# A short row block moved to the front of the second MLP, and the planner's keys laid out anew

## The chip, the cores and the metric

The kernel runs on one core of a Trainium2 chip. The metric is device time in microseconds (us) of one execution, the median of several. The engines are named as in the profile: PE is TensorE, which multiplies (PEld is its loading of weights), DVE is VectorE, ACT is ScalarE, POOL is GpSimd and SP is SyncE, whose queue issues nearly all DMAs.

## What is computed

Attention with rotary positions over 4 batches, 8 heads, 576 positions and a head size of 64, then two MLPs over its 2304 rows of 512 values. The change concerns the second MLP.

```python
x = _moe_ref(x, w_in, w_out)                       # first MLP
h = x @ w_in                                       # second MLP: (2304, 512) @ (512, 2048)
g = np.where(h > 0.0, h, np.exp(np.minimum(h, 0.0)) - 1.0)
return g @ w_out                                   # (2304, 2048) @ (2048, 512)
```

## The kernel before, in words

**Numbers in two halves.** Products of float32 matrices are made from float16 halves: each operand is split into a high half (made by ACT) and a low half (made by DVE), and three of the four products of halves are added up in PSUM.

**A planner writes the order.** The code does not issue instructions itself. It records operations with an engine, an estimated cost, the operations they wait for, the buffers they need, and a key. `Plan.run` plays these operations through once, with its own estimates of durations, and on each engine issues next the ready operation with the smallest key. What it writes is fixed: on the chip each engine works through its list in that order, whatever the real durations are. `TUNE` holds the numbers from which the keys are made (`prep`, `va`, `s`, `av`, `w1i` and so on, for parts of the attention and the conversion of weights) and three offsets (`f_dve`, `f_act`, `f_pool`) that decide which engine takes an operation that either could do. Keys of the second MLP are not in `TUNE`, but for `w2i2` and `w2o2`, which set how early the split of its two weight matrices is wanted.

**The second MLP.** Its 2304 rows are done in five row blocks (`NB2 = 5`), of 512 rows but one of 256, in the order that the list `rows` gives. For a block, `block(kb, prev_out)` does this:
- It loads the block's `y` (output of the first MLP) from DRAM, takes its maximum (L1055 on DVE, then L361 and L368 on PE across partitions) and splits it into `yhl` (L1082 on ACT, L1087 on DVE, four of each). There is one `yhl` buffer.
- First product, L1131 on PE: 16 column tiles `u`, each of 12 multiplications as wide as the block. The result of each `u` lies in one of three PSUM buffers `m`. ACT takes the exponential (L1134), DVE does L1138 and L1142, the last of which frees `m`.
- The block with `kb == 0` is done plainly: ACT and DVE split each `u` (L1145, L1149), and the second product is L1258 on PE.
- The other blocks (`fast = kb > 0`) use a scheme with seven products of half size in place of eight (L1207 on PE). It needs sums of the activations (L1114 on DVE, four for each pair of `u`), more splits (L1106 on ACT, L1109 on DVE, three for each pair), and additions behind the products (L1227 on DVE).

**Work that only the fast blocks need.** Seven of the products multiply by sums of the weights. `weight_sums(f)`, recorded right behind block 0 for f = 0 to 7, makes them on DVE (L1005, nine instructions for each f: two 512 wide, six 256 wide, one 1024 wide) with one split on ACT (L1022). They can start when the split of the second weight matrix is done: L514 on ACT and L520 on DVE, 16 of each, in a chain in which each waits for the other. A key of K2+250+f gives the weight sums precedence over the `yhl` of block 1 (key K2+400), and both stand behind the elements of block 0 (keys below zero) wherever those are ready in time.

**What sets the start of a block.** All matmuls of a block stand behind those of the block before it (`prev_out`), but the planner may put L1207 of a block between L1131 of the same block. The first multiplication of a block needs its `yhl`.

Of the kernel before, what the change touches and what calls it, by code (L numbers as in the profile page):

```python
# [20 lines left out]
    s=2, av=1, m=3, E=3, Ehl=3, et=2, qkT=4, R=2, V=1, T=1, v16=4, x=10, t=3, y=1, R2=3, yhl=1, o=3,  # L21
)
TUNE = dict(
    tab=29.669055687884857, f_dve=4735.99490362732, f_act=324.203486712257, f_pool=2991.120911549942, w1i2=87.40583026420265,
    w1o2=-84.0807171361962, dlat=823.3988909607715, kt=434.1730438572996, slack=1000000000.0, w1i=-641.8905164885398,
    w1i_s=35.2508622696485, w1o=-246.81674455296675, w1o_s=7.1899499061784695, prep0_s=62.959721309637985, prep0=574.4583012182783,
    prep=-220.89260578674165, va0=449.5098804882598, va=-814.3532604437504, vs=-249.1490854804778, tiny=688.9344832658534,
    av=505.2864272462129, ex=-841.786808518003, mx=2.580493215482753, s=334.76728659580453, tr=1002.6372188507788, w2i2=-170.54943633953243,
    w2o2=-1595.7316624510645, pt=748.6446072069625, pv=498.37407629952327,
)  # L30
LAT = {"pe": 230.0, "act": 170.0, "dve": 145.0, "pool": 200.0, "dma": 0.0, "none": 0.0}
ORDER = ("pe", "act", "dve", "pool", "dma", "none")
# [187 lines left out]
def kernel(  # L220
# [14 lines left out]
    NT, DM = out.shape  # L235
# [312 lines left out]
    tab = w2i_flat[:, 3 * QW:3 * QW + 27 * HALF]  # L548
# [407 lines left out]
    NB2 = (NT + 511) // 512  # L956
# [10 lines left out]
    def second_mlp(opened, after1, dead, scored):  # L967
# [309 lines left out]
            return prev_out  # L1277

        rows = [512] * (NB2 - 1)
        rows.insert(3, NT - 512 * (NB2 - 1))  # L1280
        done = [after1]
        for kb in range(NB2):
            done = block(kb, done)
# [28 lines left out]
    opened = op({"none": 0}, open2, list(x_ready.values()) + [o for o in W1i.ready + W1o.ready], 0)  # L1312
    dead = [o for hp in range(NP) for o in qk_ready[B - 1, hp] + [v_ready[B - 1, hp]]]
    second_mlp(opened, prev, dead, scored)

    with tc.manual_schedule():
# [55 lines left out]
```

## Time and profile before

| what | value |
|---|---|
| median of 3 runs | 1026.08 us (1023.97 to 1027.85) |
| the profiled execution, time | 1024.77 us |
| its span, first to last instruction | 1023.0 us |
| PE busy | 973.3 us |
| DVE busy | 852.3 us |
| ACT busy | 611.1 us |
| start of the first multiplication of block 0 of the second MLP | 654.70 us |

The profiled execution's own time lies 1.31 us below the median, and 1.8 us above its span. A share of busy time is a mean over stages: the second MLP takes the last third of the span, and within it each block has its own limit. So the views below are by stretch and in order of time.

### The profile page before, as it was taken

The page shows a single profiled execution, that of the slowest core. Times are in us where ns is not written, and L with a number is a line of the kernel's source. Part 1 is how long each engine was busy: PE and PEld are TensorE (multiplying, and loading weights), DVE is VectorE, ACT ScalarE, POOL GpSimd, SP SyncE. Part 2 cuts the span into 40 slices and gives each one's busy share as a digit, 9 for nine tenths or more (in the row PEclk, how much of TensorE's full clock was granted, in tenths as well). Part 3 has the DMA queues.
Part 4 walks back from the last instruction along what each step waited for, and adds up shares of the span by engine and source line. Part 5 has one row for each costly group of instructions (what it writes and reads, how often), then busy time and mean ns, then how long its engine had stood idle before and what let it go on. Part 6 is the DMA issues. An engine that isn't in the chain of part 4 may idle for free. (4 is left out here: it accounts for less than half of the span.)

```text
span 1023.0 us, 19959 instructions
## 1 busy us (share of the span) xinstructions
PE 973.3 (95%) x7818; PEld 691.4 (68%) x7818; DVE 852.3 (83%) x1686; ACT 611.1 (60%) x1184; POOL 0.4 (0%) x6
## 2 busy tenths in 40 slices
PE   3578999999999999999999999999999999998998
PEld 2455787877766678766688778644446846886477
DVE  7999998887997689999885988699698489386982
ACT  4998996565786566786563777474264155062640
POOL 0000000000000000000000000000000000000000
PEclk8579999999999999999999999999999999999999
DMA  8961548887767956778684174000100200102001
GB/s 281 314 211 43 126 70 154 164 144 110 139 114 135 176 92 119 137 159 174 139 161 139 42 214 157 27 1 0 42 1 27 57 1 12 47 7 63 1 11 33
DMA packets 200254, 103.39 MB, mean 101 GB/s; under 512 B 164064, under 2 KB 189280, under 8 KB 200160
## 3 DMA queue, kind: packets, MB, share of 16 engines
q1 hardware_dynamic: 199872, 101.62, 44.5%
q8 instruction: 61, 1.00, 0.4%
q10 hardware_dynamic: 288, 0.51, 0.2%
q14 instruction: 33, 0.27, 0.1%
HBM read 53.46 MB, written 9.44 MB: 61 GB/s over the span
## 5 line engine op out<-in xcount | busy, mean ns | idle before, releaser
L938 PE MATMUL m<-ghl,wo 128*128 128x256 f16 (+3 forms) x1728 | 199.9, 274 | 0.2 <-DVE wo L520 0.2
L1131 PE MATMUL m<-yhl,w2i 128*128 128x512 f16 (+1 forms) x960 | 188.2, 358 | 0.2
L901 PE MATMUL m<-x,wi 128*128 128x256 f16 (+3 forms) x1584 | 187.2, 271 | 1.0 <-DVE t L907 0.9
L938 PEld LDWEIGHTS <-wo 128*128 128x128 f16 x1728 | 157.0, 98 | 41.7 <-issue 11.9
L901 PEld LDWEIGHTS <-wi 128*128 128x128 f16 x1728 | 155.7, 98 | 43.5 <-issue 14.5
L1131 PEld LDWEIGHTS <-w2i 128*128 128x128 f16 x960 | 93.9, 98 | 92.9 <-issue 0.7
L720 ACT ACTIVATE E<-s,st 128x576 f32<-128x576 f32 x144 | 106.6, 741 | 52.5 <-DVE st L716 49.8
L716 DVE TENSOR_REDUCE st<-s 128x1 f32<-128x576 f32 x144 | 106.7, 748 | 4.2 <-PE s L711 4.1
L742 DVE SCALAR_TENSOR_TENSOR Ehl<-E,st,Ehl 128x576 f16<-128x576 f32 x124 | 99.5, 810 | 11.0 <-ACT Ehl L736 10.3
L736 ACT ACTIVATE Ehl<-E,st 128x576 f16<-128x576 f32 x90 | 68.3, 773 | 44.2 <-DMA et<-Ehl 15.2
L1134 ACT ACTIVATE e<-m,y_c 128x512 f32<-128x512 f32 (+1 forms) x80 | 50.9, 639 | 65.0 <-issue 35.6
L711 PE MATMUL s<-qkT 64*128 64x288 f32 (+1 forms) x480 | 81.1, 449 | 1.5 <-ACT E L720 1.4
L1207 PEld LDWEIGHTS <-g 128*128 128x128 f16 x714 | 70.3, 99 | 9.4 <-issue 0.7
L1227 DVE SCALAR_TENSOR_TENSOR x<-z,eo,x 128x256 f32<-128x256 f32 x46 | 22.0, 482 | 51.8 <-PE z L1207 51.6
L916 ACT ACTIVATE ghl<-t 128x320 f16<-128x320 f32 (+3 forms) x96 | 49.8, 524 | 21.1 <-DVE t L907 20.6
L904 ACT ACTIVATE t<-m,hsc 128x320 f32<-128x320 f32 (+3 forms) x96 | 55.5, 578 | 9.0 <-PE m L901 8.1
L711 PEld LDWEIGHTS s<-qkT 64*128 64x128 f32 (+1 forms) x480 | 42.3, 184 | 23.7 <-issue 8.3
L1207 PE MATMUL z<-wo,g 128*128 128x256 f16 x504 | 58.0, 277 | 0.0
L907 DVE SCALAR_TENSOR_TENSOR t<-t,m 128x320 f32<-128x320 f32 (+3 forms) x96 | 52.3, 547 | 5.4 <-ACT t L904 5.2
L1142 DVE SCALAR_TENSOR_TENSOR e<-m,y_c,e 128x512 f32<-128x512 f32 (+1 forms) x80 | 55.1, 690 | 0.4
L919 DVE SCALAR_TENSOR_TENSOR ghl<-t,ghl 128x320 f16<-128x320 f32 (+3 forms) x96 | 52.2, 550 | 2.2 <-ACT ghl L916 2.0
L1106 ACT ACTIVATE g<-R,y_c 128x1024 f16<-128x1024 f32 (+1 forms) x32 | 33.3, 1041 | 24.0 <-DVE R L1114 24.0
(190 smaller groups left out, 1375.8 us busy)
## 6 DMA issues: line engine op xcount, KB each, us to landing
ghl<-in_moe_w_in_dram SPq DMA_DIRECT2D x16, 512.0 KB, 6.2
R<-in_moe_w_out_dram SPq DMA_DIRECT2D x16, 512.0 KB, 4.2
wo<-in_moe_w_out_dram SPq DMA_DIRECT2D x14, 512.0 KB, 4.8
w2i<-in_moe_w_in_dram SPq DMA_DIRECT2D x14, 512.0 KB, 4.2
w2i<-in_k_dram SPq DMA_DIRECT2D x16, 256.0 KB, 3.0
w2i<-in_q_dram SPq DMA_DIRECT2D x16, 256.0 KB, 3.8
w2i<-in_v_dram SPq DMA_DIRECT2D x4, 1024.0 KB, 7.2
R<-y_d SPq DMA_DIRECT2D x8, 512.0 KB, 3.8
```

The costliest lines, as they stand in the source:

```text
L711: nc.tensor.matmul(o, X[r, t:t + (TAIL if h is None else P)], X[r, NS * w:NS * w + NS], start=True, stop=True)
L716: nc.vector.tensor_reduce(out=st["t"][:, a:a + 1], in_=take(hS[a])[:, :, 0:NS], axis=AX.XY, op=ALU.max, negate=True)
L720: nc.scalar.activation(out=take(hE[a]).rearrange("p (c f) -> p c f", c=2), in_=take(hS[a])[:, :, 0:NS], func=AF.Exp, bias=t[:, a:a + 1], s ...
L736: nc.scalar.activation(out=X16[:, 0:S], in_=take(hE[a]), func=AF.Copy, scale=r)
L742: nc.vector.scalar_tensor_tensor(out=X16[:, S:2 * S], in0=E, scalar=r, in1=X16[:, 0:S], op0=ALU.mult, op1=ALU.subtract)
L901: nc.tensor.matmul(ps, W1i.lhs(kk, u, wl), x[:, xl, 0:N], start=kk == 0 and i == 0, stop=kk == KD - 1 and i == 2)
L904: nc.scalar.activation(out=flat(ht), in_=flat(hM), func=AF.Tanh, scale=hsc[b][:, 1:2])
L907: nc.vector.scalar_tensor_tensor(out=flat(ht), in0=flat(ht), scalar=1.0, in1=flat(hM), op0=ALU.add, op1=ALU.mult)
L938: nc.tensor.matmul(ps[:, 0:N], W1o.lhs(f, d, wl), (gh, gl)[xl][:, f, g0:g0 + N], start=f == 0 and i == 0, stop=f == KF - 1 and i == 2)
L1131: nc.tensor.matmul(ps[:, 0:n], W2i.lhs(kk, u, wl), Y[:, xl, kk, 0:n], start=kk == 0 and i == 0, stop=kk == KD - 1 and i == 2)
L1142: nc.vector.scalar_tensor_tensor(out=t[:, 0:n], in0=take(hM)[:, 0:n], scalar=st["c"][:, 0:1], in1=t[:, 0:n], op0=ALU.mult, op1=ALU.max)
L1207: nc.tensor.matmul(ps, AT[A](p, gi, P * tt), BT[B](p, wl), start=p == 0 and i == 0, stop=p == 7 and i == 2)
```

## The change

The list `rows` was 512, 512, 512, 256, 512 and becomes 256, 512, 512, 512, 512. So the short block is now the plain one, and four blocks of 512 rows go through the fast scheme in place of three of 512 and one of 256. Nothing else of the code differs but 27 of the 29 numbers in `TUNE`, of which the diff here shows the first two lines.

```diff
 TUNE = dict(
-    tab=29.669055687884857, f_dve=4735.99490362732, f_act=324.203486712257, f_pool=2991.120911549942, w1i2=87.40583026420265,
-    w1o2=-84.0807171361962, dlat=823.3988909607715, kt=434.1730438572996, slack=1000000000.0, w1i=-641.8905164885398,
+    tab=-225.85054553600983, f_dve=10711.990370883193, f_act=461.965463073505, f_pool=1613.197066616173, w1i2=141.63957986767508,
+    w1o2=-371.9002375178363, dlat=823.3988909607715, kt=223.51619677805178, slack=1000000000.0, w1i=-701.3096471146007,
...
@@ -1277,7 +1277,7 @@
         rows = [512] * (NB2 - 1)
-        rows.insert(3, NT - 512 * (NB2 - 1))
+        rows.insert(0, NT - 512 * (NB2 - 1))
         done = [after1]
         for kb in range(NB2):
             done = block(kb, done)
```

On DVE, in the first product of block 0, the order was this (names are tiles; the number behind a name tells its generation, `m` is PSUM, `e` an activation, `g` its split):

```order
L1138 TENSOR_SCALAR e_8409<-e_8409 128x512
L1149 SCALAR_TENSOR_TENSOR g_8394<-e_8387,y_c,g_8394 128x512
L1142 SCALAR_TENSOR_TENSOR e_8409<-m_8374,y_c,e_8409 128x512
L1138 TENSOR_SCALAR e_8433<-e_8433 128x512
L520 SCALAR_TENSOR_TENSOR w2o<-w2o,w2o_s 128x512
L1142 SCALAR_TENSOR_TENSOR e_8433<-m_8396,y_c,e_8433 128x512
```

In the same place it is now this:

```order
L1138 TENSOR_SCALAR e_8459<-e_8459 128x256
L1149 SCALAR_TENSOR_TENSOR g_8424<-e_8416,y_c,g_8424 128x256
L1142 SCALAR_TENSOR_TENSOR e_8459<-m_8426,y_c,e_8459 128x256
L1149 SCALAR_TENSOR_TENSOR g_8424<-e_8439,y_c,g_8424 128x256
L1138 TENSOR_SCALAR e_8482<-e_8482 128x256
L520 SCALAR_TENSOR_TENSOR w2o<-w2o,w2o_s 128x512
L1142 SCALAR_TENSOR_TENSOR e_8482<-m_8446,y_c,e_8482 128x256
```

The element work of block 0 has half its width, and the work on weights (L520 here) stands between it as before, at its old width.

On DVE around the last of the four L1087, which completes the `yhl` of block 1, the order was this:

```order
L1005 TENSOR_TENSOR wo<-R_8840,wo 128x1024
L1087 SCALAR_TENSOR_TENSOR yhl_8721<-R_8151,ys_s,yhl_8721 128x512
L1005 TENSOR_TENSOR wo<-R_8858,wo 128x1024
L1005 TENSOR_TENSOR e_8912<-w2o 128x512
L1005 TENSOR_TENSOR R_8913<-e_8912 128x256
```

and it is now this:

```order
L1005 TENSOR_TENSOR wo<-R_8826,wo 128x1024
L1087 SCALAR_TENSOR_TENSOR yhl_8701<-R_8046,ys_s,yhl_8701 128x512
L1005 TENSOR_TENSOR wo<-R_8847,wo 128x1024
L1005 TENSOR_TENSOR e_8881<-w2o 128x512
L1005 TENSOR_TENSOR R_8882<-e_8881 128x256
```

The last L1087 stood behind six complete weight sums and all but the last step of a seventh; behind it one more was to be started. It stands now behind five and all but the last step of a sixth, and two are to be started behind it.

On DVE at the first elements of block 1 the order was this, with the last instruction of the weight sums ahead of the first element:

```order
L1005 TENSOR_TENSOR R_8913<-R_8913,w2o 128x256
L1005 TENSOR_TENSOR wo<-R_8913,wo 128x1024
L1138 TENSOR_SCALAR e_9024<-e_9024 128x512
L1142 SCALAR_TENSOR_TENSOR e_9024<-m_8994,y_c,e_9024 128x512
L1109 SCALAR_TENSOR_TENSOR ghl<-e_9024,y_c,ghl 128x256
```

and it is now this:

```order
L1005 TENSOR_TENSOR R_8882<-R_8882,w2o 128x256
L1142 SCALAR_TENSOR_TENSOR e_8900<-m_8868,y_c,e_8900 128x512
L1138 TENSOR_SCALAR e_8926<-e_8926 128x512
L1005 TENSOR_TENSOR R_8903<-w2o,R_8903 128x256
L1005 TENSOR_TENSOR R_8903<-R_8903,w2o 128x256
```

The last two weight sums have moved into the element work of block 1.

## Rows read from the trace of the kernel before

**Rows 1.** The page's head: span, then busy time of each engine.
```profile
span 1023.0 us, 19959 instructions
PE 973.3 (95%) x7818; PEld 691.4 (68%) x7818; DVE 852.3 (83%) x1686; ACT 611.1 (60%) x1184; POOL 0.4 (0%) x6
```

**Rows 2.** Busy time by stretch: length, each engine's us (instructions), PE clock, DMA share, GB/s.
```profile
0.00:100.00 100.00, 64.19 (x496) 43.80 (x497) 89.28 (x171) 78.99 (x158) 0.44 (x6) 0.78 0.67 217
100.00:654.70 554.70, 547.54 (x4987) 418.61 (x4984) 481.57 (x930) 377.35 (x789) 0.00 (x0) 1.00 0.66 133
654.70:696.10 41.40, 41.40 (x193) 18.78 (x192) 39.02 (x70) 28.09 (x42) 0.00 (x0) 1.00 0.01 4
895.50:925.40 29.90, 26.61 (x238) 22.98 (x236) 27.61 (x89) 18.39 (x41) 0.00 (x0) 1.00 0.08 23
925.00:930.00 5.00, 4.56 (x27) 3.46 (x28) 1.44 (x3) 0.45 (x2) 0.00 (x0) 0.66 0.30 65
```

**Rows 3.** The chain that ended last, in order: start, us, engine and line.
```profile
654.70 41.44 PE m L1131 x192
696.13 41.44 PE z L1258 x192
737.58 41.44 PE m L1131 x192
...
816.52 41.44 PE m L1131 x192
...
895.47 2.63 PE m L1131 x24
...
941.43 41.44 PE m L1131 x192
982.87 36.70 PE z L1207 x336
```

**Rows 4.** Timeline of DVE: start, us, instruction, idle before it and what ended it.
```profile
646.06 0.75 DVE L520 SCALAR_TENSOR_TENSOR w2o<-w2o,w2o_s 128x512 f16<-128x512 f32 x1 [0.48 <-ACT w2o L514]
...
657.39 0.75 DVE L520 SCALAR_TENSOR_TENSOR w2o<-w2o,w2o_s 128x512 f16<-128x512 f32 x1 [0.79 <-ACT w2o L514]
658.06 0.42 DVE L1138 TENSOR_SCALAR e<-e 128x512 f32<-128x512 f32 x1
...
726.52 0.75 DVE L1087 SCALAR_TENSOR_TENSOR yhl<-R,ys_s,yhl 128x512 f16<-128x512 f32 x1
...
740.97 0.43 DVE L1138 TENSOR_SCALAR e<-e 128x512 f32<-128x512 f32 x1 [6.26 <-ACT e L1134]
...
788.56 1.28 DVE L1109 SCALAR_TENSOR_TENSOR g<-R,y_c,g 128x1024 f16<-128x1024 f32 x1 [1.22 <-ACT g L1106]
...
897.38 0.29 DVE L1138 TENSOR_SCALAR e<-e 128x256 f32<-128x256 f32 x1 [1.38 <-ACT e L1134]
```

**Rows 5.** DVE groups by shape, whole span: count, busy us, mean ns, idle before.
```profile
L1142 DVE SCALAR_TENSOR_TENSOR e<-m,y_c,e 128x512 f32<-128x512 f32 x64 | 47.6, 744 | 0.4
L1138 DVE TENSOR_SCALAR e<-e 128x512 f32<-128x512 f32 x64 | 26.8, 418 | 11.7 <-ACT e L1134 11.7
L738 DVE TENSOR_SCALAR Ehl<-E,st 128x576 f16<-128x576 f32 x34 | 17.5, 517 | 5.0 <-DMA et<-Ehl 4.4
L1149 DVE SCALAR_TENSOR_TENSOR g<-e,y_c,g 128x512 f16<-128x512 f32 x16 | 11.9, 742 | 0.0
L1005 DVE TENSOR_TENSOR e<-w2o 128x512 f32<-128x512 f16 x16 | 11.0, 687 | 0.3
L1005 DVE TENSOR_TENSOR wo<-R,wo 128x1024 f16<-128x1024 f32 x8 | 9.7, 1217 | 1.1 <-ACT wo L1022 1.1
L1142 DVE SCALAR_TENSOR_TENSOR e<-m,y_c,e 128x256 f32<-128x256 f32 x16 | 7.4, 476 | 0.0
L1138 DVE TENSOR_SCALAR e<-e 128x256 f32<-128x256 f32 x16 | 4.4, 284 | 1.9 <-ACT e L1134 1.9
L1109 DVE SCALAR_TENSOR_TENSOR g<-e,y_c,g 128x256 f16<-128x256 f32 x6 | 2.9, 476 | 0.0
```

More of the change, by code (lines that the diff above doesn't have):

```diff
@@ L23 @@
 TUNE = dict(
-    tab=29.669055687884857, f_dve=4735.99490362732, f_act=324.203486712257, f_pool=2991.120911549942, w1i2=87.40583026420265,
-    w1o2=-84.0807171361962, dlat=823.3988909607715, kt=434.1730438572996, slack=1000000000.0, w1i=-641.8905164885398,
[L26 to L29, printed above, removed]
+    tab=-225.85054553600983, f_dve=10711.990370883193, f_act=461.965463073505, f_pool=1613.197066616173, w1i2=141.63957986767508,
+    w1o2=-371.9002375178363, dlat=823.3988909607715, kt=223.51619677805178, slack=1000000000.0, w1i=-701.3096471146007,
+    w1i_s=35.295006560150384, w1o=-288.970382295607, w1o_s=7.0294735729774125, prep0_s=80.73354021978547, prep0=711.5060984569377,
+    prep=-518.3682961524775, va0=564.1241425353367, va=-514.3532604437504, vs=-194.15244992060525, tiny=667.6726656029264,
+    av=375.7219813841871, ex=-948.7649659643791, mx=2.67698772504311, s=338.5026763982299, tr=970.8000049482956, w2i2=-219.0150182370548,
+    w2o2=-1719.6996793582275, pt=688.6530860848909, pv=337.7031782414163,
 )
```

## The prediction

> **What bounds the kernel now.** I read the page's head first: PE is busy for 95% of the span, DVE for 83% [rows 1]. Then the busy time by stretch. In the first 100 us PE is busy for 64.2 us and DVE for 89.3, so work that feeds PE sets the pace there. From 100 us to 654.7, where the second MLP begins, PE is idle for 7.2 us of 554.7 [rows 2]. Then the chain that ended last: from 654.70 it is PE almost without a break, with one exception [rows 3]. Block 0 takes 82.88 us (654.70 to 737.58), block 1 takes 78.94 (to 816.52), block 2 takes 78.95, the short block 3 takes 45.96 (895.47 to 941.43), and block 4's multiplications end 78.14 us after it begins, at 1019.57 [rows 3]. Half of a block of 512 would be 39.5, so the short block lost some 6 us. The stretch shows how: from 895.5 to 925.4 DVE is busy for 27.6 of 29.9 us and PE for 26.6 [rows 2]. In that block DVE was the limit.
>
> DVE is close to being the limit elsewhere too. In the first product of block 0 it is busy for 39.0 of 41.4 us while PE never waits [rows 2]. It does the elements of block 0 from 658.06 and between them the split and the sums of the second weight matrix. The last L1087, on which block 1 waits, starts at 726.52, some 10 us before PE comes for it at 737.58 [rows 3, 4]. The reader is to see that this margin exists only because PE takes 82.88 us over block 0.
>
> **The change part by part.** All times of the second MLP count from T, the first multiplication of block 0 (654.70 before), and the sum is made against the profiled execution's 1024.77 us.
>
> *PE's own work.* The plain block of 256 rows needs 192 multiplications of 256 columns (24 of them took 2.63 us, so 21.0) and 96 of 512 columns (192 took 41.44, so 20.7) [rows 3]: 41.8 us in place of 82.88. The fourth fast block of 512 rows takes 78.94 in place of 45.96. Together 120.7 in place of 128.8: a gain of 8.1 us, if nothing waits.
>
> *DVE's work in block 0.* At half width L1138 goes from 418 to 284 ns and L1142 from 744 to 476. L1149 at 256 columns does not occur; the same operation of L1109 at that width takes 476 against its 742 [rows 5]. That saves 0.67 us for each of 16 column tiles, 10.7 us of durations. The work on weights does not shrink: the eight sums cost the same whatever the block's width. So DVE's load falls by far less than PE's 41 us.
>
> *When is the `yhl` of block 1 done?* DVE's list is fixed, and the first element of block 0 needs PE's first result. In the short block of before, that L1138 started 1.9 us after the first multiplication (897.38 against 895.47) [rows 3, 4]. Ten of the L520 stand ahead of it. Before, the chain of L520 and L514 advanced by one in (657.39 - 646.06)/7 = 1.6 us [rows 4], so ten need 16 us. Their scale is wanted by PE after 24 of the 192 L938 of the last block of the first MLP, some 18 us before T, so this just fits and I charge nothing; if it doesn't, the start slips by a microsecond or two. From the first L1138 to the last L1087 the new list has 107 instructions: 48 for the elements of block 0, 6 L520, 4 L1087, 49 of the weight sums. Their durations, each by its group of the view by shape, sum to 54.6 us. DVE's instructions overlap a little at their ends, and some wait for ACT. Before, from the first L1138 to the last L1087, the same kind of list summed to 74.1 us and took 69.2 (658.06 to 727.27) [rows 4], a ratio of 0.934. So the last L1087 ends at T + 1.9 + 51.0 = T + 52.9. PE has finished block 0 at T + 41.8 and waits **11.1 us**, where it had 10 us in hand.
>
> *Inside block 1.* The list goes on with what is left of the weight sums (11.5 us of durations) and the fast elements of block 1 (52.0 us), 63.5 in all. Before, these 52.0 took 48.9 us (740.97 to 789.84) [rows 4], 0.94 with their waits, so DVE now needs 59.7 and is done at T + 112.6. PE cannot run ahead: three buffers `m` are freed only by L1142. After DVE's last split, PE still has 222 of the 336 L1207 (0.109 us each by 36.70/336 [rows 3]) and one exchange across partitions, 0.8 us more (78.94 - 41.44 - 36.70): 25.0 us. Block 1 ends at T + 137.6, which is 84.7 after its start in place of 78.94: **5.8 us** more.
>
> *After that* three fast blocks follow as before, 78.95, 78.95 and 78.14. The multiplications end at T + 373.7; before it was T + 364.87. In sum -8.1 + 11.1 + 5.8 = **+8.8 us**. For bounds I take the ratio of elapsed time to durations from 0.91 (hardly a wait) to 0.97 (most instructions depend on the one ahead): +5.6 to +12.6.
>
> *The first part*, with its keys laid out anew. The number of multiplications on PE is the same. DVE gets rid of 4.5 us of durations in all (five L738 of 517 ns [rows 5] among them), which ACT takes over. Summed in the same way, DVE's list up to the 16th maximum of scores is 3.9 us shorter, but up to the last split of the first weight matrix 5.9 longer. So T moves by between -4 and +6. PE's idle 7.2 us after the first 100 us leave little to gain there [rows 2]. I take -1.
>
> *DMAs.* Two more stores of the output are issued, because the blocks meet the batches at other rows; like the others they lie beside PE. The loads of `y` for block 1 are wanted before T either way. I charge nothing; a late load would delay L1055 and add to the wait above.
>
> *PE's clock.* When PE resumed after the waits of the short block (3.3 us together), the clock was 0.66 of full speed from 925 to 930 us, where the two levels are 1.2 and 2.4 GHz; the price was 0.34 of 4.56 us, 1.5 us [rows 2]. After a wait of 11 us the same must be expected. But block 1's first column tile at half speed takes 5.2 us, and DVE still has the end of one weight sum and the beginnings of two to do (5.7 us of durations, 5.3 elapsed) before it looks at that tile, so I charge nothing. The Trainium skill (TensorE: Matmul & The Clock Gate, Part 1) says that the array's clock falls to the lower level when the engine idles and comes back as it works. The trace agrees with its 0.66; by the page the change adds one more such stretch.
>
> So 1024.77 + 8.8 - 1 = 1032.6 for an execution like the profiled one. The median of the runs shown is 1.3 above it, which gives 1034.
>
> **The rivals.** *PE is the bound and DVE keeps up (faster).* Then only the 8.1 us count, and the time is 1024.77 - 8.1 - 1 + 1.3 = 1017. For it speaks PE's 95% [rows 1]. It decides itself at the last L1087: if its end comes before T + 41.8, the gain is whole. That needs 11 of DVE's 51 us to vanish; nothing in the list before it is optional, and the first element can't start before T. Chance 6%. The Trainium skill (Perfetto Trace Analysis, Identifying the Most-Contended Engine) takes the engine with the highest occupancy as the one to optimize; by that rule this rival would be the forecast. The stretch 895.5 to 925.4, with DVE at 92% and PE waiting, speaks against reading it over the whole span.
>
> *The new keys give back what the blocks lose (no change).* If the first 100 us, where PE idles for 35.8 [rows 2], shrink by 5 us or more, or DVE's ratio is at its low end and T at -4, the time is 1022 to 1031, say 1028. For it: the shorter list up to the 16th maximum. Against it: the longer one to the last split. Chance 23%.
>
> *The waits feed each other (slower still).* If PE stays at the lower clock in block 1, its first product takes up to 82.9 us in place of 41.44 and becomes the limit again; a third of it at that level adds 14, of which the 5.8 us of waiting are cover. That gives 1042. Against it: from 895.5 to 925.4 PE waited a little again and again, and its clock was 1.00 [rows 2]. Chance 13%. My forecast has 58%.
>
> **How the numbers follow.** The likeliest case gives 1034. The range goes down to 1025, which takes in most of the second rival, and up to 1042, which holds the upper bounds of DVE's ratio and of T (+12.6 and +4). A measurement can tell about 0.5% from no change, 5 us: faster below 1021, slower above 1031. Faster has the first rival and a little of the second, 0.08. The forecast lies for its larger part above 1031, and with the third rival slower has 0.67. No measurable change has 0.25.
>
> **What would show it.** Right: PE idle for about 11 us ahead of the first L1131 of block 1, ended by DVE L1087; block 1 some 85 us long with DVE busy for nearly all of its first 60; no wait in the four fast blocks' rows of L1207 after that; T within 4 us of 654.7; a clock below 1.00 where PE resumes. Wrong: the last L1087 of block 1 before the last L1258, or a T that has moved by more than the blocks have. In the first case the sum of DVE's list is wrong, in the second the keys of the attention decide the sign.

## The result, and the profile after

| | before | after |
|---|---|---|
| median | 1026.96 us (1023.97 to 1027.95, 4 runs) | 1032.99 us (1031.84 to 1033.85, 4 runs) |
| profiled execution: time, span | 1024.77, 1023.0 us | 1033.85, 1032.1 us |
| T, first multiplication of block 0 of the second MLP | 654.70 | 658.25 |
| last multiplication ends | T + 364.87 | T + 370.39 |

The ratio is 1.0075, with a 95% interval of 1.0055 to 1.0095: the changed kernel is slower, by about 6 us of the medians. The forecast was 1034. In the profiled executions the second MLP has grown by 5.5 us and the part ahead of it by 3.55. These 9.1 us are more than the 6.0 between the medians: the profiled execution after is the slowest of its four, the one before lies 2.2 us below its median.

The page's head shows nearly nothing, in the form of [rows 1]: PE is still busy for 95% of the span and DVE for 83%.

```profile
span 1032.1 us, 20140 instructions
PE 975.7 (95%) x7890; PEld 701.0 (68%) x7890; DVE 858.7 (83%) x1687; ACT 616.1 (60%) x1191; POOL 0.4 (0%) x6
```

The chain that ended last, as in [rows 3], gives the blocks: T, then the starts of blocks 2, 3 and 4 and the end.

```profile
658.25 1.32 PE m L1131 x12
...
792.61 41.44 PE m L1131 x192
...
871.56 41.44 PE m L1131 x192
...
950.51 41.44 PE m L1131 x192
991.95 36.69 PE z L1207 x336
```

From block 2 on every block takes 78.95 us and the end comes 236.03 us after 792.61, as PE's own work asks. So all that the second MLP loses lies ahead of T + 134.36. PE's timeline shows where (start, us, instruction, count, idle before it and what ended it):

```profile
700.61 2.32 PE L1131 MATMUL m<-yhl,w2i 128*128 128x512 f16 x10
...
710.05 19.08 PE L1131 MATMUL m<-yhl,w2i 128*128 128x512 f16 x74 [7.12 <-DVE yhl L1087]
...
747.71 7.93 PE L1131 MATMUL m<-yhl,w2i 128*128 128x512 f16 x36 [1.24 <-DVE e L1142]
...
767.81 5.63 PE L1207 MATMUL z<-wo,g 128*128 128x256 f16 x50 [0.60 <-DVE g L1109]
```

Block 0 is done at 700.61 = T + 42.4. PE runs ten multiplications of block 1 with the quarters of `yhl` that are there, then stands for 7.12 us until the last L1087. DVE's timeline has the other side:

```profile
660.10 0.29 DVE L1138 TENSOR_SCALAR e<-e 128x256 f32<-128x256 f32 x1 [0.47 <-ACT e L1134]
...
709.26 0.74 DVE L1087 SCALAR_TENSOR_TENSOR yhl<-R,ys_s,yhl 128x512 f16<-128x512 f32 x1
...
766.48 1.27 DVE L1109 SCALAR_TENSOR_TENSOR g<-R,y_c,g 128x1024 f16<-128x1024 f32 x1
```

The busy time by stretch (columns as in [rows 2]) closes it: from its first L1138 to the last L1087, and from there to the last split of block 1, DVE is busy for 48.69 of 49.90 and 57.06 of 57.75 us. It waits for nobody; PE waits for it.

```profile
0.00:100.00 100.00, 65.86 (x490) 45.69 (x492) 85.87 (x166) 79.05 (x157) 0.44 (x6) 0.81 0.68 217
100.00:658.25 558.25, 549.17 (x4992) 419.56 (x4989) 482.08 (x935) 383.74 (x803) 0.00 (x0) 1.00 0.65 131
660.10:710.00 49.90, 42.31 (x282) 27.32 (x280) 48.69 (x108) 26.43 (x48) 0.00 (x0) 0.96 0.03 11
710.00:767.75 57.75, 55.73 (x300) 29.92 (x299) 57.06 (x110) 30.63 (x44) 0.00 (x0) 0.95 0.01 3
700.00:725.00 25.00, 17.88 (x70) 7.39 (x69) 24.14 (x49) 9.33 (x13) 0.00 (x0) 0.80 0.05 20
```

### The profile page after: what moved, and what is told of

Its sections match the earlier page's. It is cut to its first block, busy times and chain, and to the rows that moved or that the text cites. A ratio compares the mean times of both kernels' runs of the same rounds, so it can differ in the third digit from the quotient of the medians.

```text
span 1032.1 us, 20140 instructions
## 1 busy us (share of the span) xinstructions
PE 975.7 (95%) x7890; PEld 701.0 (68%) x7890; DVE 858.7 (83%) x1687; ACT 616.1 (60%) x1191; POOL 0.4 (0%) x6
## 4 chain that ended last, share of the span: by engine, by line
PE 68%; DVE 19%; DMA 7%; ACT 3%; issue 2%; SPq 1%; ACTq 0%; DVEq 0%
PE m L938 15%; PE z L1207 14%; PE m L1131 13%; PE m L901 12%; PE s L711 6%; PE av L833 3%; DMA et<-Ehl 3%; DVE st L716 2%; DMA w2i<-in_v_dram 2%; DVE R L1005 2%; DVE Ehl L742 1%; DVE e L1142 1%; PE m L599 1%; DVE t L907 1%; PE av L843 1%
## 5 line engine op out<-in xcount | busy, mean ns | idle before, releaser
L1131 PE MATMUL m<-yhl,w2i 128*128 128x512 f16 (+1 forms) x960 | 191.4, 361 | 9.1 <-DVE yhl L1087 7.1
L901 PEld LDWEIGHTS <-wi 128*128 128x128 f16 x1728 | 156.0, 98 | 42.7 <-issue 13.6
L1131 PEld LDWEIGHTS <-w2i 128*128 128x128 f16 x960 | 94.6, 99 | 104.0 <-issue 14.2
L736 ACT ACTIVATE Ehl<-E,st 128x576 f16<-128x576 f32 x95 | 72.5, 773 | 31.4 <-DMA et<-Ehl 13.6
L1207 PEld LDWEIGHTS <-g 128*128 128x128 f16 x816 | 79.6, 98 | 10.7 <-DVE g L1109 0.9
L1227 DVE SCALAR_TENSOR_TENSOR x<-z,eo,x 128x256 f32<-128x256 f32 x52 | 24.8, 482 | 54.4 <-PE z L1207 54.3
L1207 PE MATMUL z<-wo,g 128*128 128x256 f16 x576 | 64.4, 273 | 0.6 <-DVE g L1109 0.6
L907 DVE SCALAR_TENSOR_TENSOR t<-t,m 128x320 f32<-128x320 f32 (+3 forms) x96 | 52.2, 546 | 5.8 <-ACT t L904 5.5
L1142 DVE SCALAR_TENSOR_TENSOR e<-m,y_c,e 128x512 f32<-128x512 f32 (+1 forms) x80 | 54.9, 690 | 0.3
L919 DVE SCALAR_TENSOR_TENSOR ghl<-t,ghl 128x320 f16<-128x320 f32 (+3 forms) x96 | 52.2, 549 | 3.3 <-ACT ghl L916 3.1
L1207 PEld LDWEIGHTS <-ghl 128*128 128x128 f16 x480 | 46.6, 98 | 6.7 <-issue 0.2
```

Of the source, the lines that this page charges most:

```text
L736: nc.scalar.activation(out=X16[:, 0:S], in_=take(hE[a]), func=AF.Copy, scale=r)
L901: nc.tensor.matmul(ps, W1i.lhs(kk, u, wl), x[:, xl, 0:N], start=kk == 0 and i == 0, stop=kk == KD - 1 and i == 2)
L907: nc.vector.scalar_tensor_tensor(out=flat(ht), in0=flat(ht), scalar=1.0, in1=flat(hM), op0=ALU.add, op1=ALU.mult)
L1131: nc.tensor.matmul(ps[:, 0:n], W2i.lhs(kk, u, wl), Y[:, xl, kk, 0:n], start=kk == 0 and i == 0, stop=kk == KD - 1 and i == 2)
L1142: nc.vector.scalar_tensor_tensor(out=t[:, 0:n], in0=take(hM)[:, 0:n], scalar=st["c"][:, 0:1], in1=t[:, 0:n], op0=ALU.mult, op1=ALU.max)
L1207: nc.tensor.matmul(ps, AT[A](p, gi, P * tt), BT[B](p, wl), start=p == 0 and i == 0, stop=p == 7 and i == 2)
```

## The experiments

The theory: PE's work beside which DVE splits and sums the second weight matrix has been halved, that work of DVE has not, and PE waits for the difference. The rivals: the new keys, PE's clock, the order in which DVE does its work, the form of the short block.

Read from the profiled execution of each kernel, in us from that kernel's own T. Medians and ratios against the kernel before stand with each experiment; a difference to the changed kernel compares medians of different series of runs, in which the kernel before had medians from 1024.95 to 1026.96 us.

| kernel | T | last `yhl` of block 1 done | last split of block 1 done | block 2 begins | multiplications end |
|---|---|---|---|---|---|
| before | 654.70 | 72.6 | 135.1 | 161.8 | 364.9 |
| after | 658.25 | 51.8 | 109.5 | 134.4 | 370.4 |
| e1, row order alone | 655.70 | 52.2 | 110.0 | 143.3 | 379.3 |
| e3, half of the sums | 660.58 | 38.6 | 94.2 | 120.7 | 356.7 |
| e4, `yhl` first | 660.24 | 31.2 | 102.7 | 136.7 | 372.7 |
| e5, second half on POOL | 657.99 | 35.6 | 99.2 | 137.2 | 373.3 |
| e9, the same, all sums early | 655.79 | 39.2 | 112.4 | 139.8 | 375.8 |
| e10, more on POOL, all early | 657.70 | 42.7 | 116.4 | 141.3 | 377.3 |
| e11, on POOL, last four early | 656.09 | 35.5 | 110.0 | 134.8 | 370.9 |

**The two parts of the change apart.**

```diff
 e1: TUNE as before
-        rows.insert(3, NT - 512 * (NB2 - 1))
+        rows.insert(0, NT - 512 * (NB2 - 1))
 e2: TUNE as after, rows.insert(3, ...) as before
```

> The short block comes first, and all keys of TUNE stay as before. Theory (the row order costs about 5.5 us by DVE's work on weights, the new keys 3.5 us by the attention): the first multiplication of block 0 stays at 654.7 us (within 1), PE waits 7 to 11 us ahead of block 1 for the last L1087, and the time is 1024.8 + 5.5 to 7, that is 1030 to 1032, a ratio of 1.005 to 1.007. DVE's list from its first L1138 to the last L1087 of block 1 sums to 55.4 us of durations here (54.6 in the changed kernel), with 11 of the L520 in it in place of 6. Rival 1 (the whole loss comes from the keys): 1017, as if PE's own work counted alone. Rival 2 (the keys were laid out for this row order and without them it is worse): over 1035, by the five additional L520 in block 0.

> The new keys with the old row order. Theory: the first multiplication of block 0 comes at about 658.3 us as in the changed kernel, the second MLP takes as long as before from there (multiplications end 364.9 us after it), so the time is 1028 to 1029, a ratio of 1.003 to 1.004. DVE's list from its first L1138 to the last L1087 of block 1 sums to 72.4 us (74.1 before), so PE does not wait for it. Rival (the 3.5 us belong to the row order, not to the keys): 1025, ratio 1.000.

Measured: e1 1041.03 us against 1026.32, ratio 1.014 (1.0118 to 1.0163); e2 1026.25, ratio 1.0009 (0.9992 to 1.0026). The first theory of the split is wrong in both halves; rival 2 of e1 and the rival of e2 came true. The row order alone costs 14.7 us and not 6, and the keys alone cost nothing that can be measured, so the 3.55 us ahead of T are not theirs as a price. With the short block first the keys win back 8.9 us of the second MLP (379.3 against 370.4 in the table). PE's timeline of e1 has a wait that the changed kernel has not:

```profile
707.98 7.67 PE L1131 MATMUL m<-yhl,w2i 128*128 128x512 f16 x26 [8.45 <-DVE yhl L1087]
...
770.78 0.59 PE L1207 MATMUL z<-wo,g 128*128 128x256 f16 x2 [5.75 <-ACT wo L1022]
...
772.04 5.15 PE L1207 MATMUL z<-wo,g 128*128 128x256 f16 x25 [0.67 <-DVE wo L1005]
```

In e1 five more L520 stand in DVE's list from the first L1138 of block 0 on, and four steps of the first weight sum that the changed kernel has ahead of it. (A weight sum f needs only the slices f and f + 8 of the split, not all 16, so it can start this early.) DVE is at its last split of block 1 as early as in the changed kernel (T + 110.0 and T + 109.5), but nine L1005 of the last sums come behind it, the last ending at T + 116.3, and PE's seven products need them. So the new keys act through what they leave for DVE to do behind T.

**DVE's amount, without its order or PE's work.**

```diff
 e3: each weight sum without T2 and T4
-            o = op({"dve": 4 * c_dve(QD)}, second, [o], k, use=[hs, hd], port=True)
-            o = op({"act": c_act(1024)}, hi, [o], k, use=[hs])
-            t_ops.append(op({"dve": c_dve(1024)}, lo, [o], k, use=[hs], port=True))
+            o = op({"act": c_act(512)}, hi, [o], k, use=[hs, hd])
+            t_ops.append(op({"dve": c_dve(512)}, lo, [o], k, use=[hs], port=True))
```

> The changed kernel with half of DVE's weight sums left out: of each of the eight sums only two of the four parts are made (and split), so T2 and T4 hold old weights and the second MLP's output is wrong where they are used. PE's instructions are the same. DVE loses about 20 us of durations: from its first L1138 to the last L1087 of block 1 its list sums to 41.8 us in place of 54.6, and to the last split of block 1 to 58.5 more in place of 64.4. Theory (DVE's amount of work beside the halved block 0 is what PE waits for): the last L1087 ends at T + 1.9 + 38 = T + 40, PE's wait ahead of block 1 shrinks from 7.1 to at most 1 us, block 1 takes 79 us, and the second MLP is 13 us shorter than in the changed kernel: about 1020, below the kernel before, ratio 0.995. Rival (PE's clock or its own work sets the time of block 1): the time stays within 2 us of the changed kernel, 1031 to 1033.

Measured: 1019.46 us, ratio 0.9928 (0.9904 to 0.9951), 13.5 us below the changed kernel. In the whole second MLP PE waits for nothing (the view of waits has no row), and the chain is PE alone:

```profile
660.58 19.68 PE m L1131 x180
...
702.30 41.44 PE m L1131 x192
...
781.25 41.44 PE m L1131 x192
...
980.58 36.70 PE z L1207 x336
```

The second MLP takes 356.70 us, 8.2 less than before. That is the gain of PE's own work that the change would have brought. Up to the last split of block 1 DVE's list is 18.7 us shorter here (41.8 and 58.5 in place of 54.6 and 64.4); ACT's split of the sums is half as wide too. The rival that PE's own work sets the time of block 1 falls with it: PE has the same multiplications, a few of them in another order. Its clock stays at 1.00 through the second MLP of e3, where PE does not wait, so what a lower clock would cost is not settled here but by DVE's idle time (see the part on the prediction).

**DVE's order, without its amount.**

```diff
 e4:
-            k = K2 + 250 + f
+            k = K2 + 450 + f
```

> The changed kernel with the key of the weight sums raised above that of the yhl of block 1, so that DVE makes the yhl first and the weight sums after it; nothing is left out. From its first L1138 to the last L1087 of block 1 DVE's list now sums to 34.1 us in place of 54.6, and from there to the last split of block 1 to 78.1 in place of 64.4. Theory (the amount of DVE's work counts, not its order): the wait of 7.1 us ahead of block 1 goes, but the last split of block 1 still comes at T + 1.9 + 0.91 x 112 = T + 104 (109.5 in the changed kernel), and two weight sums stand behind it, so PE waits inside block 1 instead and the second MLP gains 0 to 5 us: 1027 to 1033. Rival (the order of the L1087 behind the weight sums is the cause): PE never waits, block 1 takes 79 us, and the time is about 1020.

Measured: 1037.05 us, ratio 1.009 (1.0065 to 1.0114): 4 us above the changed kernel, though the intervals of the two ratios overlap, and its second MLP is 2.3 us longer. That is outside both expectations, if nearer to the theory's. The `yhl` is there 20 us earlier and PE does not wait for it. The view of waits shows what came in its place (us in total, times, longest):

```profile
PE m L1131 <- DVE e L1142: 6.2, 5, 2.3
PE z L1207 <- ACT wo L1022: 4.8, 1, 4.8
PE z L1207 <- DVE wo L1005: 2.0, 2, 1.3
```

Of these 13.0 us 12.4 lie inside block 1, in place of 7.1 ahead of it and 2.0 inside. So the place of the L1087 behind the weight sums is not the cause; what was missed is the same as in e1: ten steps of the last two sums stand behind the last split.

**A part of the sums on POOL.** POOL is idle in the second MLP, and e3 says what 18.7 us less on DVE's list is worth.

```diff
 e5: base after; e5b: the same on base e1
-            o = op({"dve": 4 * c_dve(QD)}, second, [o], k, use=[hs, hd], port=True)
+            o = op({"pool": 4 * c_pool(QD)}, second, [o], k, use=[hs, hd], port=True)
 e9: e5, and
-            k = K2 + 250 + f
+            k = -8.5e4 + f
 e10: e9, and lo (1024 wide) on POOL
 e11: e5, and
-            k = K2 + 250 + f
+            k = K2 + 250 + f if f < 4 else -8.5e4 + f
```

> The changed kernel, complete, with four of the nine instructions of each weight sum (the four 256 wide of its second half) on POOL, which is idle there, in place of DVE. DVE's list from its first L1138 to the last L1087 of block 1 sums to 34.1 us in place of 54.6. Theory (PE waits for the amount of DVE's work): the last L1087 ends by T + 35, ahead of the end of block 0 at T + 42, there is no wait ahead of block 1, and the time is that of the kernel with half of the sums left out, 1019 to 1022, ratio 0.993 to 0.996. No row of the traces so far prices a tensor_tensor on POOL; it fits if the 32 instructions take under about 1.6 us each (51 us). Rival (POOL is slow, or slows DVE while it works): PE waits at the first L1207 that multiplies by the sums, or DVE's rows of 512 and 1024 columns grow above 687 and 1217 ns, and the time is 1030 or more.

> The same move of work to POOL with the short block first and the old keys. With the row order alone the old keys cost 8 us against the new ones. Theory (the keys matter only through what DVE has to do beside block 0 and block 1: five L520 and the last weight sum): with DVE relieved the difference between old and new keys goes, and the time is within 3 us of the variant with the new keys, 1018 to 1023. Rival (the new keys do something for this row order that has nothing to do with DVE's amount): 1027 to 1030.

> The changed kernel with the second half of each weight sum on POOL, as before, and the key of the weight sums lowered to -8.5e4, ahead of the sums of activations (L1114) that took the R2 buffers from the last two of them; no weight sum stands behind block 1's elements now. DVE's list sums to 35.8 + 69.2 us from its first L1138 to the last split of block 1. With the 6.3 us by which its rows grew beside POOL that is 111.3, by 0.91 elapsed 101, so the last split comes at T + 103 and block 1 ends 25 us later at T + 128, against T + 134.4 in the changed kernel. Theory (the last two sums were late because of their place in the list, and the sum of DVE's work then sets the end): 1025 to 1029, no wait for L1022 or L1005 above 1 us. Rival (DVE and POOL disturb each other wherever the sums stand): 1033 or more.

> As the one above, with the last step of each weight sum (1024 wide, 1.22 us on DVE) on POOL too. DVE's list sums to 33.6 + 62.6 = 96.2 us; with 6 to 12 us of growth beside POOL 102 to 108, elapsed 93 to 98, so its last split comes at T + 95 to T + 100, where PE needs it at T + 96. Theory (the amount on DVE): block 1 ends at T + 121 to T + 125, the second MLP takes 357 to 361 us, 1018 to 1023, ratio 0.992 to 0.997. Rival (POOL's wide step holds the R2 buffers longer, and PE waits for the last sums at L1207): 1028 or more. No row prices the 1024-wide step on POOL; by the 0.8 us for 256 columns it would take some 3 us.

> The changed kernel with the second half of each weight sum on POOL, and the early key of -8.5e4 only for the last four sums, so that the split of the second weight matrix (L520) keeps its place ahead of them. DVE's list sums to 34.1 + 70.9 us, with 6.3 of growth beside POOL 111, elapsed 101: its last split comes at T + 103, block 1 ends 25 us later at T + 128, and three blocks of 78.9 to 78.1 follow. Theory (once neither the split nor the sums are late by their place, the amount on DVE alone sets the end): the second MLP takes 364 us, no wait for L520, L1022 or L1005 above 2 us, 1024 to 1029, ratio 0.998 to 1.003. Rival (POOL beside DVE costs more than the rows of before show): 1033 or more.

Measured: e5 1038.98 us, ratio 1.0119 (1.0098 to 1.014); e5b 1046.28, 1.019 (1.0167 to 1.0213); e9 1040.44, 1.014 (1.0118 to 1.0161); e10 1041.2, 1.0143 (1.0121 to 1.0166); e11 1035.83, 1.0108 (1.0091 to 1.0126). All five theories missed: none is faster than the changed kernel, and the difference between old and new keys did not go with the work on POOL (e5b is 7.3 us above e5). The times of the rivals came true in e5, e9, e10 and e11, though e10's not by its mechanism: PE waits there for L1142 and not for the last sums. e5b is above its rival too: sixteen steps of the sums stand behind its last split of block 1, ten in e5, and PE waits 20.0 us for L1022 and L1005.

The table and the waits show two reasons. In e5 the `yhl` is early and there is no wait ahead of block 1, but the last two sums stand behind block 1's own sums (L1114), which have the smaller key and use the same buffers, and PE waits for them at L1207 (7.13 us for the L1022 of one, 4 more behind it). In e9 nothing is late in block 1, which takes 78.95 us, but the early sums stand ahead of the split L520, and block 0 waits, for 12.7 us in all:

```profile
700.32 0.59 PE L1258 MATMUL z<-w2o,g 128*128 128x512 f16 x1 [4.83 <-DVE w2o L520]
...
706.07 0.58 PE L1258 MATMUL z<-w2o,g 128*128 128x512 f16 x1 [3.93 <-DVE w2o L520]
...
711.83 4.78 PE L1258 MATMUL z<-w2o,g 128*128 128x512 f16 x13 [3.94 <-DVE w2o L520]
```

e11 has neither fault, and its second MLP is as long as the changed kernel's (370.9 against 370.4). Yet DVE's last split comes at T + 110.0, as in the changed kernel, with 13.6 us of work (32 x 0.425) taken from DVE. PE waits for L1142, 10.5 us in six pieces. The groups by shape show why. POOL's own instructions are in the first two rows, then come DVE's, which were 688, 1217, 425 and 282 ns in the changed kernel.

```profile
L1005 POOL TENSOR_TENSOR R<-w2o,R 128x256 f32<-128x256 f16 x16 | 16.4, 1024 | 713.9 <-DVE R L1005 706.7 <-ACT yhl L1082 6.5
L1005 POOL TENSOR_TENSOR R<-R,w2o 128x256 f32<-128x256 f32 x16 | 11.9, 744 | 1.3
...
L1005 DVE TENSOR_TENSOR e<-w2o 128x512 f32<-128x512 f16 x16 | 11.9, 744 | 1.0 <-DMA out_dram<-e 0.7
...
L1005 DVE TENSOR_TENSOR wo<-R,wo 128x1024 f16<-128x1024 f32 x8 | 10.7, 1333 | 0.0
...
L1005 DVE TENSOR_TENSOR R<-e 128x256 f32<-128x256 f32 x16 | 10.0, 624 | 0.5
...
L1138 DVE TENSOR_SCALAR e<-e 128x256 f32<-128x256 f32 x16 | 5.7, 359 | 0.4 <-ACT e L1134 0.2
```

These four groups alone give back 6.2 us. Taken over all rows from the first L1138 to the last split of block 1, each against its mean in the changed kernel, the growth is 9.8 us. DVE, never idle in this stretch in the changed kernel, waits 3.0 us in e11, and with fewer instructions some 1.7 us less of them overlaps. Together that is more than the 13.6 us that POOL took. So e9 to e11 were priced too low twice: growth of 6.3 us was taken over from e5, where the same count gives 7.8 (11.1 in e9, 17.3 in e10), and no waits. In e10 PE waits 14.2 us for L1142, and POOL's step of 1024 columns takes 2316 ns.

**The form of the short block, and its place.** The other side of the change: the fast block of 256 rows that it removed.

```diff
 e6, e7:
-            fast = kb > 0
+            fast = kb > 0 and rows[kb] == 512
 e6, e8: rows.insert(4, ...); e7: rows.insert(3, ...) as before; TUNE as before
```

> Old keys, a plain block of 512 rows first as in the kernel before, three fast blocks of 512, and the short block of 256 last, done plainly. Theory: the cover for the weight work is that of before (the last L1087 comes 10 us ahead of PE), and the short block takes 41.8 us of PE's own work in place of the 45.96 that it takes as a fast block with DVE at its limit. Second MLP: 82.88 + 3 x 78.95 + 41.8 = 361.5 us against 364.87 before: 3.4 us less, 1023, ratio 0.996 to 0.998. Rival (a plain block behind a fast one waits for its yhl or for the buffers of the activations, or the longer stores at the end show): 1026 or more.

> Old keys and the old row order (512, 512, 512, 256, 512); the short block in fourth place is done plainly in place of fast, nothing else changes. Theory: the form of the short block costs 4 us, not its place, so this gains what the variant with the short block last gains: second MLP 82.88 + 2 x 78.95 + 41.8 + 78.14 = 360.7 us against 364.87, 1022, ratio 0.995 to 0.997. Rival (the fast block behind it inherits the wait, as DVE's elements of a plain block also take 16 x (284 + 476 + 477) ns and its yhl comes late): 1025 to 1027, ratio 0.999 to 1.001.

> Old keys, the short block moved from fourth to last place and still fast. Theory (the form of the short block costs 4 us, its place nothing): 45.96 us for it wherever it stands, the time is that of before, 1025 to 1028, ratio 0.999 to 1.001, above both variants in which the short block is plain. Rival (the place counts: no block behind it competes for DVE): 1022 to 1024 like those.

Measured: e6 1024.1 us, ratio 0.9976 (0.9962 to 0.999); e7 1023.14, 0.997 (0.9951 to 0.9988); e8 1026.87, 1.0011 (0.9995 to 1.0027). As expected: the form counts, and the place costs nothing that can be measured. e7's chain gives the short block 41.68 us (898.19 to 939.87), where it was 45.96 in [rows 3]:

```profile
818.42 41.44 PE m L1131 x192
...
898.19 20.96 PE m L1131 x192
919.15 20.72 PE z L1258 x96
939.87 41.44 PE m L1131 x192
```

So e6 and e7 beat the kernel before by some 2 to 3 us and the changed one by 9 to 10: they take the short block away from the fast scheme, and keep 82.88 us of block 0 above DVE's work on the weights.

## Why the prediction was right, step by step

*PE's own work, -8.1 us.* Right: e3, in which nothing waits, shows -8.2.

*When the `yhl` of block 1 is done.* Right in the mechanism, a little off in size. DVE's 54.6 us of durations took 49.9 (660.10 to 710.00), a ratio of 0.914 where I took 0.934. Waits do not explain the difference, though the prediction calls its bound of 0.91 "hardly a wait": DVE waited in neither stretch. What carries over is the overlap of each instruction with the next: 4.9 us over 122 instructions before, 4.7 over 107 after, some 0.04 each. The new list has shorter instructions (0.51 us in the mean, 0.61 before), so the same overlap is a larger share. By it the 54.6 us would have given 50.3. The first L1138 came at T + 1.85 (predicted T + 1.9), the last L1087 ended at T + 51.75 (T + 52.9).

*The wait of 11.1 us.* Mis-sized by the same 1.2, by 0.6 us more for block 0 itself, and because a step was left out: PE need not have the whole `yhl` to begin. From 700.61 to 710.05 it stood for 7.12 us and worked for 2.32 ahead of time.

*Inside block 1.* The last split ended at T + 109.5, predicted T + 112.6, again by the ratio: the stretch took 57.75 us for 64.4 of durations (0.90), where 0.94 was taken from a stretch with waits in it, and 63.5 of durations. From it to block 2 PE needed 24.9 us, predicted 25.0. Block 2 began at T + 134.36 in place of T + 137.6, and the rest took 236.03 us against 236.04.

*The sum.* +5.5 where +8.8 stood, just under the lower bound of +5.6: the term of DVE's ratio was the one that was mis-sized, and PE's early start on block 1 the step that was missing.

*The first part.* Wrong in sign for the profiled execution: +3.55 where -1 stood, within its bounds of -4 to +6. e2 shows that the keys alone have no measurable price, while T scatters from 655.8 to 660.6 over the seven executions whose list on PE up to T is that of the changed kernel, and from 654.5 to 656.6 over the four with that of the kernel before; the means, 658.1 and 655.5, leave room for a loss of some 2.6 us that belongs to neither part alone. PE's idle time ahead of T is the same, 43.0 and 43.2 us by the first two stretches of [rows 2] and those above; it is PE's busy time that grew, from 611.7 to 615.0 at 5483 and 5482 instructions. Why stays open. That 1034 stood against 1033 is in part luck: in the profiled execution the second MLP was forecast 3.3 us too long and the part ahead of it 4.6 too short. Between the medians the change cost 6.0 us, where 7.9 was forecast.

*DMAs and the clock, both nothing.* Right. The granted clock was 0.80 in the mean from 700 to 725 us, for a part of it at the lower of its two levels behind the 7.12 us in which PE stood, and the 74 multiplications behind the wait took 19.08 us, where at 41.44 us for 192 they take 16.0. But DVE was not idle once between 660.10 and 767.75, so PE's slower start cost nothing.

*The rivals.* That PE is the bound was wrong, and by a distance: for PE not to wait in block 1, DVE's last split would have had to come some 14 us earlier (T + 109.5, where T + 41.8 + 78.94 - 25.0 = T + 95.7 was needed). In e3 it came at T + 94.2. That the new keys give it back was half true: they give back 8.9 us of the second MLP, as e1 shows, but the list that was summed was already the one with the new keys. That waits feed each other did not happen: blocks 2 to 4 wait for nothing.

## What to carry to other kernels

A block that runs at its matrix engine's pace may be the cover for another engine's one-time work; before it is made shorter or moved, sum that other engine's list over the stretch, with everything that does not shrink with the block. With an engine that never idles, moving work within its list only moved the wait (e4). Less work on it helped where the work was gone (e3), and not where it went to an engine that slows the first (e5 and e9 to e11). Where a planner fixes the order, numbers that seem to belong to an earlier stage can decide how much of a later stage's work is already done when it begins.

## What the runs showed of the hardware

DVE and POOL are not independent. With POOL working beside it, DVE's 256-column `tensor_tensor` from one buffer to another (L1005) went from 425 to 624 ns in e11 and 715 in e10. In e11 the timelines part them: the nine of the 16 that ran beside a POOL instruction took 779 ns in the mean, the other seven 425. L1142, which reads one operand from PSUM, did not grow: at 256 columns, in the same block 0, it went from 474 to 477 ns in e11 and 479 in e10. The Trainium skill (SBUF — State Buffer, Who interferes with whom) says that a DVE instruction with two SBUF inputs contends with a GpSimd instruction that reads SBUF, and one with a single SBUF input outside the two-port modes does not; these rows agree. L1138, which reads one SBUF operand, grew too (282 to 359 ns); 512 columns cost it 418 ns, so 0.53 ns for each further column where L1142 needs 1.05, but in which mode it ran no row shows. POOL took 744 to 1024 ns for what DVE does alone in 421 to 425.

Instructions that follow each other on DVE overlap in the records, except where one needs the buffer of the one ahead. Of the 107 of the changed kernel (54.6 us of durations in 49.9, 0.914), 72 overlap the one ahead by 0.08 us in the mean, whether that is 256, 512 or 1024 wide. The other 34 stand some 0.035 us behind it; all but one are steps of a weight sum on the buffer of the step ahead. Here L1142 starts 0.08 us before L520 has ended, and the second L1005, which takes what the first one made, 0.04 us after it:

```profile
660.31 0.75 DVE L520 SCALAR_TENSOR_TENSOR w2o<-w2o,w2o_s 128x512 f16<-128x512 f32 x1
660.98 0.48 DVE L1142 SCALAR_TENSOR_TENSOR e<-m,y_c,e 128x256 f32<-128x256 f32 x1
661.37 0.41 DVE L1005 TENSOR_TENSOR R<-w2o,R 128x256 f32<-128x256 f16 x1
661.82 0.43 DVE L1005 TENSOR_TENSOR R<-R,w2o 128x256 f32<-128x256 f32 x1
```

So a ratio of time to durations, taken from one list, does not carry over to a list of shorter instructions.
